# A mixture-of-experts kernel: each call's first block gets its second layer in the next call's code, and the next weights are fetched there

## Chip, cores, metric

One core of a Trainium2 chip. The metric is the device time in microseconds (us) from launch to the last output. The input is fixed, so the tokens of each expert are the same in every run.

## What is computed

Attention over q, k, v of 4 x 8 heads x 768 positions x 64, where each position sees its neighbours within 16 places and one summary (max of k, mean of v) of each block of 32. Its output, 3072 tokens of 512, goes through a mixture of 8 experts with one expert per token:

```python
logits = np.einsum('bsd,de->bse', x, w_gate)
local_gate = 1.0 / (1.0 + np.exp(-np.einsum('bsd,de->bse', x, w_local).squeeze(-1)))
...
            fresh_e = int(np.argmax(logits[b, s]))
            if s == 0 or local_gate[b, s] < 0.5:
                e = fresh_e
            else:
                e = prev_e if prev_e >= 0 else fresh_e
            prev_e = e
...
            h = np.maximum(x[b, s] @ w1[e], 0.0)
            out[b, s] = p[e] * (h @ w2[e])
```

w1[e] is 512 x 1024 and w2[e] 1024 x 512, so 4 MB of fp32 for one expert. The expert of a token can be that of the token before it, so the routing is known only on the chip.

## The kernel before, in words

Up to about 205 us the core does the attention, with the routing and the first expert blocks woven in by a hand-written planner (`flow`, `small`, `until`): small routing steps are generators that yield the name of the engine they use, and the constants C_T, C_LONG and the like say how much time a step takes up. After it, the work is a plain list.

Tokens are sorted by expert into blocks of 128. A *call* is one piece of code for 3 blocks (a 3-call), 2 blocks (a 2-call) or 1 block (`single`) of one expert. Which blocks are in use is known on the chip alone, so the calls stand in nests of branches: run's line 1525 for 3-calls 1 to 7, line 1533 for eight 2-calls, line 1539 for eight singles. When the count is reached, every engine jumps out of the nest, past the code of the calls that are not taken, and then catches up the semaphores that the skipped code would have counted. With this input the list is: early blocks of experts 2 and 3 within the attention; five 3-calls, three of expert 3 and two of expert 4; one 2-call of expert 2; one single of expert 6. Experts 0 and 6 also have a *few* part: up to 32 left-over tokens of an expert in a small block with its own weights (`few`, lines 1258 to 1295). The first few part stands behind 3-call 0, the second between the 3-calls and the 2-calls.

In a call (`blocks`), each fp32 product is three matmuls of split numbers, high times high, high times low and low times high. The first layer runs over 8 column groups f and 4 row groups c (lines 1187 to 1189, 96 matmuls), ACT applies the relu (line 1193) and DVE makes the low part (line 1195). The second layer runs block after block, 24 matmuls each (lines 1159 to 1161). After each block `store` scales by the gate (ACT line 1168 or DVE line 1171) and POOL writes the rows to their tokens by an indirect DMA (line 1172). Between the matmuls of the second layer stand the steps that get the next call ready: transposes of its tokens (`mid`, PE line 1138), and the *splits* of the next weights (`split`): ACT casts the high part (line 1113), DVE (line 1116) or POOL (line 1121) subtracts to get the low part. W1's four chunks are split in the first block's second layer, W2's in the last block's:

```python
SPLIT_BY = ("VGVV", "VGVG")
...
PW1, PW2 = (0, 2, 4, 6), (2, 4, 6, 7)
```

A split is under a branch on "the next call has new weights". Behind a matrix's last chunk SP fetches the weights after next into the staging tile `stg` (`refill`, `fetch` line 1109), two issues of 1 MB for each matrix. In all there are five such fetches; the last one names expert 0 by default and no call uses it.

The routing turns positions into gather lists: DVE writes the one-hot `bp` (lines 1042 to 1072) from `at`, a table of SLOTS block starts, and PE multiplies by it (line 1077).

Of the kernel before, what the change touches and what calls it, by code (L numbers as in the profile page):

```python
# [19 lines left out]
P = 128  # L20
# [15 lines left out]
N3, N2, N1, MORE = 8, 8, 8, 2  # L36
# [5 lines left out]
AT1 = AT2 + 2 * (N2 + MORE)  # L42
SLOTS = AT1 + N1 + MORE
# [29 lines left out]
C_LONG = {"LONG": 1.0, "LONGER": 1.8}  # L73
# [4 lines left out]
class Kernel:  # L78
# [755 lines left out]
    def finish(self):  # L834
# [146 lines left out]
        for i in range(2):  # L981
            yield "DVE"
            v.tensor_scalar(out=ends[:, i:i + 1], in0=pos[:, i, E:E + 1], scalar1=float(CALL), scalar2=None, op0=ALU.max)
# [5 lines left out]
        v.tensor_scalar(out=ends[:, 2:3], in0=pos[:, 2, E:E + 1], scalar1=float(CALL), scalar2=None, op0=ALU.max)  # L989
# [54 lines left out]
        yield "LONG"  # L1044
# [4 lines left out]
        for i in range(3):  # L1049
            yield "LONG"  # L1050
            v.tensor_tensor(out=bp[:, :, n * i:n * i + n], in0=eq, in1=self.p3[:, :, i, :].to_broadcast([P, NT, n]), op=ALU.mult)
# [56 lines left out]
    def fetch(self, dst, which, c0, c1, e):  # L1108
        self.nc.sync.dma_start(out=dst, in_=self.w[which][bass.ds(e, 1), :, c0:c1].rearrange("o p c -> (o p) c"))
# [14 lines left out]
    def gather(self, i):  # L1124
        t = self.xg[(i % 2, (i - EARLY) % CALL, (i - AT2) % 2, 0)[(i >= EARLY) + (i >= AT2) + (i >= AT1)]]
# [30 lines left out]
    def mm(self, ps, ah, al, w, first, last):  # L1156
        nc = self.nc
        wh, wl = w
        nc.tensor.matmul(out=ps, lhsT=ah, rhs=wh, start=first, stop=False)  # L1159
        nc.tensor.matmul(out=ps, lhsT=ah, rhs=wl, start=False, stop=False)  # L1160
        nc.tensor.matmul(out=ps, lhsT=al, rhs=wh, start=False, stop=last)  # L1161
# [13 lines left out]
    def blocks(self, i, k, mid, w1, w2, between=None):  # L1175
# [5 lines left out]
        for f in range(0, FT, per):  # L1181
            ps = self.bank("s")[:, 0:per * n].rearrange("p (f t) -> p f t", f=per)
            for j in range(per):
                for c in range(KT):
                    c0 = self.w1_at(f + j, c)
                    wh, wl = [w[0][:, c0:c0 + P] for w in (self.hi, self.lo)]
                    nc.tensor.matmul(out=ps[:, j], lhsT=wh, rhs=xh[c], start=(c == 0), stop=False)  # L1187
                    nc.tensor.matmul(out=ps[:, j], lhsT=wh, rhs=xl[c], start=False, stop=False)  # L1188
                    nc.tensor.matmul(out=ps[:, j], lhsT=wl, rhs=xh[c], start=False, stop=(c == KT - 1))  # L1189
# [6 lines left out]
        last = FT * (k - 1)  # L1196
        pm = PM if i else PM0
        for half in range(k):
            yp = self.bank("a")
            s = slice(P * half, P * half + P)  # L1200
            for f in range(FT):
                self.mm(yp, hT[:, f, 0, s], hT[:, f, 1, s], [x[1][:, f * DM:f * DM + DM] for x in (self.hi, self.lo)], f == 0, f == FT - 1)
                yield
                j = FT * half + f
# [4 lines left out]
                if between and j == FT * k - 4:  # L1209
                    between()  # L1210
                for at, w in (PW1, w1), ([last + x for x in PW2], w2):
                    if j in at:
                        w(*(q for q in range(4) if at[q] == j))
            self.store(yp, i + half, i < EARLY or half == k - 1)
        yield

    def single(self, i, mid, w1, w2):
# [16 lines left out]
        mm1(1, (2, 3))  # L1234
        w1(0, 1)
# [13 lines left out]
        self.store(yp, i)  # L1249
# [49 lines left out]
    def run(self):  # L1299
# [105 lines left out]
        def refill(w, nxt):  # L1405
            for h in range(2):
                self.fetch(st["stage"][w][:, 2048 * h:2048 * h + 2048], w, 2048 * h, 2048 * h + 2048, nxt)
# [6 lines left out]
        def calls(n, blocks, lane):  # L1414

            r = {}

            def start(s):
                while "words" not in st:
                    self.small(1, True)  # L1420
                if s not in r:
                    r[s] = reg(s, (ENG.SP, ENG.Activation, ENG.DVE, ENG.Pool), 1), reg(LANES + s, (ENG.SP,), E - 1)
                return r[s]

            def weights(w, chunks):
# [8 lines left out]
                new, nxt = start(lane)  # L1434
# [15 lines left out]
            return mid, lambda *chunks: weights(0, chunks), lambda *chunks: weights(1, chunks)  # L1450
# [9 lines left out]
        with ExitStack() as ctx:  # L1460
# [20 lines left out]
            def more_hT():  # L1481
# [3 lines left out]

            rest = chain(first, more_hT(), self.blocks(2, 2, *calls(4, 2, LANE1)), self.blocks(4, 2, *calls(EARLY, CALL, 0)),
                         self.blocks(EARLY, CALL, *calls(EARLY + CALL, CALL, 1), lambda: few_tx(0)))
# [24 lines left out]
            def few(j):  # L1512
                with tc.If(used[j] > 0):
# [8 lines left out]
            used = [few_reg(j, (ENG.PE, ENG.Activation, ENG.DVE, ENG.Pool)) for j in range(FEWS)]  # L1522
            few(0)
            n3, n2, n1 = [reg(2 * LANES + i, mybir.ALL_ENGINES, CALL * n) for i, n in enumerate((N3, N2, N1))]
            with ExitStack() as c:
                for n in range(1, N3):
                    c.enter_context(tc.If(n3 > CALL * n))
                    i = EARLY + CALL * n
                    for _ in self.blocks(i, CALL, *calls(i + CALL, CALL, n + 1)):
                        pass  # L1530
            few_tx(1)
            few(1)
            with ExitStack() as c:
                for n in range(N2):
                    c.enter_context(tc.If(n2 > CALL * n))
                    i = AT2 + 2 * n
                    for _ in self.blocks(i, 2, *calls(i + 2, 2, LANE2 + n + 1)):
                        pass
            with ExitStack() as c:
                for n in range(N1):  # L1540
                    c.enter_context(tc.If(n1 > CALL * n))
                    self.single(AT1 + n, *calls(AT1 + n + 1, 1, LANE3 + n + 1))

# [11 lines left out]
def consts():  # L1555
# [5 lines left out]
    at = [*range(EARLY, AT2), *(EARLY + CALL * n + h for n in range(N2 + MORE) for h in range(2)),  # L1561
          *(EARLY + CALL * n for n in range(N1 + MORE))]
# [71 lines left out]
```

## Time and profile before

| what | value |
|---|---|
| runs | 456.85, 456.86, 458.81 us; median 456.86 |
| profiled execution | 458.84 us, span first to last instruction 456.6 us |
| mean granted TensorE clock | 0.975 |
| busy share of the span | PE 92%, weight loads 80%, DVE 51%, ACT 42%, POOL 42% |
| weight fetches `stg` | 20 issues of 1 MB, median 7.1 us to landing |
| few-part weights `few_w` | 8 issues of 1 MB, median 8.5 us to landing |

The span is that of one profiled execution. Its time stands 1.98 us above the median of the runs. PE's busy share is the share of the span in which a matmul was in flight, so a PE at half clock counts as busy too. The granted clock is 1.00 at 2.4 GHz and 0.50 at 1.2 GHz. Rows with a q behind the engine's name (PEldq, DVEq) are the engine's sequencer: branches, semaphores, DMA issues.

### The profile page before, as it was taken

The page shows a single profiled execution, that of the slowest core. Times are in us where ns is not written, and L with a number is a line of the kernel's source. Part 1 is how long each engine was busy: PE and PEld are TensorE (multiplying, and loading weights), DVE is VectorE, ACT ScalarE, POOL GpSimd, SP SyncE. Part 2 cuts the span into 40 slices and gives each one's busy share as a digit, 9 for nine tenths or more (in the row PEclk, how much of TensorE's full clock was granted, in tenths as well). Part 3 has the DMA queues.
Part 4 walks back from the last instruction along what each step waited for, and adds up shares of the span by engine and source line. Part 5 has one row for each costly group of instructions (what it writes and reads, how often), then busy time and mean ns, then how long its engine had stood idle before and what let it go on. Part 6 is the DMA issues. An engine that isn't in the chain of part 4 may idle for free. (4 is left out here: it accounts for less than half of the span.)

```text
span 456.6 us, 11396 instructions
## 1 busy us (share of the span) xinstructions
PE 420.8 (92%) x4225; PEld 364.5 (80%) x4226; DVE 231.9 (51%) x581; ACT 190.3 (42%) x454; POOL 193.2 (42%) x287
## 2 busy tenths in 40 slices
PE   8799989899999999998999999999999999699084
PEld 4678868678897898988987988988988987597063
DVE  4766787998776789749331231244221244217001
ACT  4868787787752246221111221253320253127111
POOL 3687676688405209822033012034612024607601
PEclk9989999999999999999999999999999999899678
DMA  8999989997162900852484612006612006432901
GB/s 310 393 349 388 403 281 399 380 382 260 47 231 66 407 36 25 291 211 77 151 317 162 261 29 87 24 24 254 190 64 92 24 24 217 158 120 69 378 25 53
DMA packets 22855, 87.45 MB, mean 192 GB/s; under 512 B 2766, under 2 KB 3408, under 8 KB 19184
## 3 DMA queue, kind: packets, MB, share of 16 engines
q1 hardware_dynamic: 18176, 71.93, 42.3%
q0 software_dynamic: 4448, 14.29, 9.5%
q8 instruction: 39, 0.64, 0.6%
q14 instruction: 48, 0.39, 0.3%
q10 hardware_dynamic: 144, 0.20, 0.1%
HBM read 73.83 MB, written 12.71 MB: 190 GB/s over the span
## 5 line engine op out<-in xcount | busy, mean ns | idle before, releaser
L1187 PE MATMUL bs<-xT,h 128*128 128x384 f32 (+1 forms) x288 | 91.7, 319 | 0.8 <-issue 0.8
L1188 PE MATMUL bs<-xT,h 128*128 128x384 f32 (+1 forms) x288 | 89.9, 312 | 0.0
L1189 PE MATMUL bs<-xT,l 128*128 128x384 f32 (+1 forms) x288 | 89.8, 312 | 0.0
L1159 PE MATMUL ba<-h,hT 128*128 128x512 f32 x192 | 78.1, 407 | 0.0
L1127 POOL DMA_INDIRECT xg<-x_dram,gidx x30 | 30.5, 1018 | 106.3 <-PE bt L1138 55.7
L1161 PE MATMUL ba<-h,hT 128*128 128x512 f32 x192 | 75.4, 393 | 0.0
L1160 PE MATMUL ba<-l,hT 128*128 128x512 f32 x192 | 75.1, 391 | 0.0
L1195 DVE SCALAR_TENSOR_TENSOR hT<-bs,hT 128x384 fp32r<-128x384 f32 (+1 forms) x56 | 33.3, 594 | 82.1 <-ACT hT L1193 80.6
L1193 ACT ACTIVATE hT<-bs 128x384 fp32r<-128x384 f32 (+1 forms) x56 | 29.3, 523 | 100.9 <-PE bs L1189 99.0
L1187 PEld LDWEIGHTS bs<-xT,h 128*128 128x128 f32 x288 | 54.5, 189 | 2.1 <-issue 1.7
L1188 PEld LDWEIGHTS bs<-xT,h 128*128 128x128 f32 x288 | 54.6, 190 | 0.3
L1189 PEld LDWEIGHTS bs<-xT,l 128*128 128x128 f32 x288 | 54.5, 189 | 0.0
L1121 POOL TENSOR_TENSOR l<-stg,h 128x256 fp32r<-128x256 f32 x48 | 47.9, 1040 | 15.2 <-ACT h L1113 15.2
L317 ACT ACTIVATE pr<-bs,nm 128x120 f32<-128x120 f32 x192 | 50.9, 355 | 7.3 <-DVE nm L309 6.9
L1172 POOL DMA_INDIRECT out_dram<-yo,sidx x24 | 25.1, 1045 | 58.9 <-ACT yo L1168 12.3
L1161 PEld LDWEIGHTS ba<-h,hT 128*128 128x128 f32 x192 | 36.1, 188 | 7.9
L1160 PEld LDWEIGHTS ba<-l,hT 128*128 128x128 f32 x192 | 36.2, 189 | 6.3
L1159 PEld LDWEIGHTS ba<-h,hT 128*128 128x128 f32 x192 | 36.2, 188 | 6.3
L1113 ACT CAST h<-stg 128x1024 fp32r<-128x1024 f32 x32 | 33.2, 1050 | 17.7 <-PE ba L1161 16.6
L328 ACT COPY pt<-bt 124x384 f32<-124x384 f32 x64 | 27.8, 491 | 11.9 <-PE bt L327 11.8
L1116 DVE TENSOR_TENSOR l<-stg,h 128x1024 fp32r<-128x1024 f32 x20 | 26.1, 1303 | 13.2 <-ACT h L1113 13.1
L274 POOL COPY vw<-vs 24x384 f32<-24x384 f32 x64 | 30.3, 514 | 5.2 <-ACT vs L269 2.9
(264 smaller groups left out, 635.7 us busy)
## 6 DMA issues: line engine op xcount, KB each, us to landing
stg<-in_w SPq DMA_DIRECT2D x20, 1024.0 KB, 7.1
vw<-in_vW SPq DMA_DIRECT2D x16, 780.0 KB, 7.0
few_w<-in_w SPq DMA_DIRECT2D x8, 1024.0 KB, 8.5
kp<-in_kT SPq DMA_DIRECT2D x16, 384.0 KB, 6.2
q<-in_qT SPq DMA_DIRECT2D x16, 384.0 KB, 6.9
vt<-in_vT SPq DMA_DIRECT2D x16, 384.0 KB, 7.0
x_dram<-xs SPq DMA_DIRECT2D x8, 768.0 KB, 5.5
wst<-in_w SPq DMA_DIRECT2D x8, 512.0 KB, 7.0
```

The costliest lines, as they stand in the source:

```text
L274: nc.gpsimd.tensor_copy(out=vw[n % 3][WL:W, t:t + NW // 4, :, 0:D], in_=vs.to_broadcast([NB, NW // 4, 2, D]))
L317: nc.scalar.activation(out=pr[:, h, u, 0:W], in_=sp[:, h, u, :], func=AF.Exp, bias=nm[:, h, u:u + 1], scale=1.0)
L1113: self.nc.scalar.copy(out=hi, in_=src)
L1121: eng.tensor_tensor(out=lo[:, p], in0=src[:, p], in1=hi[:, p].bitcast(F32), op=ALU.subtract)
L1127: self.nc.gpsimd.indirect_dma_start(out=t, out_offset=None, in_=rows, in_offset=bass.IndirectOffsetOnAxis(ap=self.gidx[:, i:i + 1], axis=0))
L1159: nc.tensor.matmul(out=ps, lhsT=ah, rhs=wh, start=first, stop=False)
L1160: nc.tensor.matmul(out=ps, lhsT=ah, rhs=wl, start=False, stop=False)
L1161: nc.tensor.matmul(out=ps, lhsT=al, rhs=wh, start=False, stop=last)
L1187: nc.tensor.matmul(out=ps[:, j], lhsT=wh, rhs=xh[c], start=(c == 0), stop=False)
L1188: nc.tensor.matmul(out=ps[:, j], lhsT=wh, rhs=xl[c], start=False, stop=False)
L1189: nc.tensor.matmul(out=ps[:, j], lhsT=wl, rhs=xh[c], start=False, stop=(c == KT - 1))
L1195: nc.vector.scalar_tensor_tensor(out=l, in0=ps, scalar=0.0, in1=h.bitcast(F32), op0=ALU.max, op1=ALU.subtract)
```

## The change

The second layer of a call's first block leaves that call. It is now run by `left_over` as the first thing in the next call's code (in the code of the next 3-call, 2-call or single, whichever is taken), and W2's splits stand between its matmuls. A call's own second layer has the other blocks alone; W1's splits stand in the first of these. The next weights are fetched by `late`: SP issues all four pieces once the first group (f = 0) of the call's first layer is done on PE, by a dependency made by hand. `single` does this behind its first layer's last matmul. 3-calls 0 and 1 are always run (SURE = 2), and the second few part stands behind 3-call 1. ACT, in place of DVE, scales the left-over block and the single. The slot table grows by two (SLOTS 66 to 68): in front of the 2-calls and of the singles stands one more, the left-over block of the nest before. Two planner constants change and the one-hot steps are rated LONGER.

```diff
-N3, N2, N1, MORE = 8, 8, 8, 2
+N3, N2, N1, MORE, SURE = 8, 8, 8, 2, 2
...
-C_LONG = {"LONG": 1.0, "LONGER": 1.8}
+C_LONG = {"LONG": 0.9, "LONGER": 1.7}
...
-        yield "LONG"
+        yield "LONGER"
...
+    def left_over(self, i, w2=None):
+
+        def hook(f):
+            if w2 and f in PW2:
+                w2(PW2.index(f))
+
+        yield from self.second_layer(0, i, True, hook)
...
+            if refill and f == 0:
+                refill(ins)
+        halves = range(w2 is None, k)
+        pm, last = PM if i else PM0, FT * (len(halves) - 1)
+        for half in halves:
...
+            yield from self.second_layer(half, i + half, i < EARLY or half == k - 1, hook)
...
+        def late(lane):
+
+            def weights(after):
+                have_all()
+                new, nxt = reg(lane, (ENG.SP,), 1), reg(LANES + lane, (ENG.SP,), E - 1)
                 with tc.If(new > 0):
-                    split(w, chunks)
-                    if chunks[-1] == NCH - 1:
-                        refill(w, nxt)
+                    for w in range(2):
+                        refill(w, nxt, after)
...
+            def call3(n, between=None):
+                i = EARLY + CALL * n
+                if n:
+                    yield from self.left_over(i - CALL, splits(1, n))
+                yield from self.blocks(i, CALL, *calls(i + CALL, CALL, n + 1)[:2], None, between, late(n))
+
+            def call2(n):
+                i = AT2 + 1 + 2 * n
+                yield from self.left_over(i - (2 if n else 1), splits(1, LANE2 + n))
+                yield from self.blocks(i, 2, *calls(i + 2, 2, LANE2 + n + 1)[:2], None, None, late(LANE2 + n))
...
+            emit(call3(1, between1))
+            few(1)
...
+            def call1(n):
+                i = AT1 + 1 + n
+                self.single(i, *calls(i + 1, 1, LANE3 + n + 1), late(LANE3 + n))
+
+            with tc.If(n1 > 0) as some:
+                emit(self.left_over(AT1, splits(1, LANE3)))
+                call1(0)
...
+            with some.Else():
+                emit(self.left_over(AT1))
```

PE on leaving the 2-calls. `h_121` and `l_123` are the high and low parts of W2, `h_120` and `l_122` those of W1; L1533 and L1539 are the branches of the 2-calls and the singles. Before:

```order
L1159 MATMUL ba<-h_121,hT 128x512
L1160 MATMUL ba<-l_123,hT 128x512
L1161 MATMUL ba<-h_121,hT 128x512
L1435 UNCONDITIONAL_BRANCH
L1533 UNCONDITIONAL_BRANCH
L1533 UNCONDITIONAL_BRANCH [waits PE_49] x8
L1539 COMPARE_AND_BRANCH
L1159 MATMUL bs<-h_120,xT 128x512 [waits DVE_49,PE_49,Activation_49]
L1160 MATMUL bs<-l_122,xT 128x512 [waits DVE_49,Pool_49]
L1161 MATMUL bs<-h_120,xT 128x512 [waits DVE_49]
```

After (the branches are L1585 and, for the singles, L1594):

```order
L1454 UNCONDITIONAL_BRANCH
L1160 MATMUL ba<-l_123,hT 128x512 [waits Pool_49]
L1161 MATMUL ba<-h_121,hT 128x512
L1585 UNCONDITIONAL_BRANCH
L1585 UNCONDITIONAL_BRANCH [waits PE_49] x8
L1594 COMPARE_AND_BRANCH
L1159 MATMUL ba<-h_121,hT 128x512 [waits DVE_49,Activation_49]
L1160 MATMUL ba<-l_123,hT 128x512 [waits DVE_49]
L1161 MATMUL ba<-h_121,hT 128x512 [waits DVE_49]
L1159 MATMUL ba<-h_121,hT 128x512
L1160 MATMUL ba<-l_123,hT 128x512
```

What followed the jump before was the single's first layer, which needs the new W1 split by POOL; now it is 24 matmuls by the old W2, waiting for DVE and ACT only, with the splits of the new W2 among them.

SP around the first 2-call, its weight issues (`stg_3009` is W1's staging, `stg_3010` W2's). Before, behind the last chunk of each matrix in the 2-call's second layer:

```order
L1435 COMPARE_AND_BRANCH
L1109 ISA
L1109 DMA stg_3009<-in_w 128x2048 [waits DMAHW1_49,DVE_49,DMAHW5_49,Activation_49,Pool_49]
L1109 ISA
L1109 DMA stg_3009<-in_w 128x2048 [waits DMAHW6_49,DMAHW2_49,DVE_49]
L1435 UNCONDITIONAL_BRANCH
L1435 UNCONDITIONAL_BRANCH [waits DMAHW5_49,DMAHW6_49]
L1435 COMPARE_AND_BRANCH
...
L1435 COMPARE_AND_BRANCH
L1109 ISA
L1109 DMA stg_3010<-in_w 128x2048 [waits DMAHW3_49,DVE_49,DMAHW7_49,Activation_49,Pool_49]
L1109 ISA
L1109 DMA stg_3010<-in_w 128x2048 [waits DMAHW0_49,DVE_49,DMAHW4_49,Activation_49,Pool_49]
```

After, at the head of the same call, where `PE_49` among the waits is the first layer's first group:

```order
L1585 COMPARE_AND_BRANCH
L1422 TENSOR_LOAD words
...
L1454 UNCONDITIONAL_BRANCH x4
L1464 COMPARE_AND_BRANCH
L1109 ISA
L1109 DMA stg_3009<-in_w 128x2048 [waits DVE_49,DMAHW1_49,PE_49,DMAHW5_49,Activation_49,Pool_49]
L1109 ISA
L1109 DMA stg_3009<-in_w 128x2048 [waits DMAHW2_49,DMAHW6_49,DVE_49,Activation_49]
L1109 ISA
L1109 DMA stg_3010<-in_w 128x2048 [waits DMAHW3_49,DVE_49,DMAHW7_49,Activation_49,Pool_49]
L1109 ISA
L1109 DMA stg_3010<-in_w 128x2048 [waits DMAHW0_49,DVE_49,DMAHW4_49,Activation_49,Pool_49]
```

The four issues moved from two places in the second layer, each behind its own branch, to one place ahead of it, behind one branch and one wait for PE.

## Rows read from the trace of the kernel before

**Rows 1.** The page, span in 40 slices: granted TensorE clock in tenths.
```profile
PEclk9989999999999999999999999999999999899678
```

**Rows 2.** PE's waits: tile, line, releaser: us in total, times, longest.
```profile
PE bs L1159 <- DVEq L1533: 7.7, 1, 7.7
PE bs L1160 <- POOLq L1533: 4.8, 1, 4.8
PE bt L1265 <- DMA xg<-x_dram,gidx: 3.5, 1, 3.5
PE bt L1077 <- DVE bp L1072: 1.8, 1, 1.8
```

**Rows 3.** Timeline of PE, ACT, DVE: start us, length us, what [idle <-releaser].
```profile
387.49 0.39 PE L1161 MATMUL ba<-h,hT 128*128 128x512 f32 x1
...
398.44 0.39 PE L1187 MATMUL bs<-xT,h 128*128 128x256 f32 x1
...
410.06 0.40 PE L1159 MATMUL ba<-h,hT 128*128 128x512 f32 x1
...
421.70 0.39 PE L1161 MATMUL ba<-h,hT 128*128 128x512 f32 x1
...
435.31 0.80 PE L1160 MATMUL bs<-l,xT 128*128 128x512 f32 x1 [4.77 <-POOLq L1533]
...
449.54 0.39 PE L1161 MATMUL ba<-h,hT 128*128 128x512 f32 x1
...
390.70 0.69 ACT L1168 ACTIVATE yo<-ba,psort 128x512 f32<-128x512 f32 x1 [1.62 <-DMA out_dram<-yo,sidx]
...
421.89 1.23 DVE L1116 TENSOR_TENSOR l<-stg,h 128x1024 fp32r<-128x1024 f32 x1 [1.42 <-ACT h L1113]
```

**Rows 4.** Busy time by stretch; after POOL: granted clock, DMA share, GB/s.
```profile
241.80:249.80 8.00, 7.04 (x144) 5.56 (x144) 1.22 (x4) 1.24 (x3) 2.01 (x3) 1.00 0.39 129
249.80:284.30 34.50, 34.49 (x180) 31.44 (x181) 8.04 (x13) 5.70 (x11) 5.83 (x6) 1.00 0.36 141
392.30:395.70 3.40, 3.40 (x64) 3.19 (x63) 0.00 (x0) 0.28 (x1) 3.40 (x6) 0.51 0.21 77
422.10:435.30 13.20, 0.76 (x1) 0.29 (x1) 1.02 (x1) 1.63 (x2) 7.37 (x10) 0.67 0.92 349
436.00:440.00 4.00, 4.00 (x11) 3.14 (x10) 0.00 (x0) 0.00 (x0) 0.00 (x0) 0.50 0.01 4
440.00:450.00 10.00, 9.93 (x49) 7.83 (x48) 2.11 (x4) 2.96 (x5) 0.98 (x1) 0.99 0.06 17
```

**Rows 5.** PE's branches leaving 3-calls, 2-calls: ns min/median/max, first to last start.
```profile
L1525 PEldq COMPARE_BRANCH  x2: 184/3626/7068, 383.7 to 390.9; - x2
...
L1533 PEldq COMPARE_BRANCH  x2: 3586/4865/6144, 417.9 to 422.3; - x2
```

**Rows 6.** DMA issues (ns of the issue) and us to landing.
```profile
L1109 SPq DMA_DIRECT2D few_w<-in_w x4: 333/333/342, 246.4 to 249.2; - x4
...
DMA to landing us min/median/max: 5.0/8.5/10.9
...
L1172 POOL DMA_INDIRECT out_dram<-yo,sidx x1: 1026/1026/1026, 380.6 to 380.6; - x1
...
DMA to landing us min/median/max: 10.0/10.0/10.0
...
L1109 SPq DMA_DIRECT2D stg<-in_w x2: 343/439/535, 419.3 to 419.9; - x2
...
L1109 SPq DMA_DIRECT2D stg<-in_w x2: 332/332/332, 425.8 to 428.5; - x2
...
DMA to landing us min/median/max: 6.9/7.1/7.2
...
L1172 POOL DMA_INDIRECT out_dram<-yo,sidx x1: 1008/1008/1008, 451.0 to 451.0; - x1
...
DMA to landing us min/median/max: 3.2/3.2/3.2
```

More of the change, by code (lines that the diff above doesn't have):

```diff
@@ L1160, in mm @@
         nc.tensor.matmul(out=ps, lhsT=ah, rhs=wl, start=False, stop=False)
-        nc.tensor.matmul(out=ps, lhsT=al, rhs=wh, start=False, stop=last)
+        self.last_mm = nc.tensor.matmul(out=ps, lhsT=al, rhs=wh, start=False, stop=last).ins
     def store(self, yp, i, act=False):
@@ L1188, in blocks @@
                     nc.tensor.matmul(out=ps[:, j], lhsT=wh, rhs=xl[c], start=False, stop=False)
-                    nc.tensor.matmul(out=ps[:, j], lhsT=wl, rhs=xh[c], start=False, stop=(c == KT - 1))
+                    ins = nc.tensor.matmul(out=ps[:, j], lhsT=wl, rhs=xh[c], start=False, stop=(c == KT - 1)).ins
                     if k > 2 or c % 2:
@@ L1195, in blocks, with hook @@
             nc.vector.scalar_tensor_tensor(out=l, in0=ps, scalar=0.0, in1=h.bitcast(F32), op0=ALU.max, op1=ALU.subtract)
[L1196 to L1204, printed above, removed]
+            if refill and f == 0:
[3 more added lines that the diff above has]
+        for half in halves:
+            def hook(f):
+                j = FT * (half - halves[0]) + f
                 if i > EARLY and j == pm[0]:
@@ L1412, in split, with have_all, splits, weights @@
                 self.split(w, q * CH, q * CH + CH, st["stage"][w][:, q * CH:q * CH + CH], eng)
[L1414 to L1425, printed above, removed]
+        def have_all():
+            while "words" not in st:
+                self.small(1, True)
+        def splits(w, lane):
+            new = []
+            def weights(*chunks):
                 if lane is None:
@@ L1433, in weights, with calls @@
                     return
-                new, nxt = start(lane)
+                if not new:
+                    have_all()
+                    new.append(reg(lane, (ENG.Activation, ENG.DVE, ENG.Pool), 1))
+                with tc.If(new[0] > 0):
+                    split(w, chunks)
+            return weights
+        def late(lane):
+            def weights(after):
+                have_all()
+                new, nxt = reg(lane, (ENG.SP,), 1), reg(LANES + lane, (ENG.SP,), E - 1)
                 with tc.If(new > 0):
-                    split(w, chunks)
-                    if chunks[-1] == NCH - 1:
-                        refill(w, nxt)
+                    for w in range(2):
+                        refill(w, nxt, after)
+            return weights
+        def calls(n, blocks, lane):
             def mid(half):
@@ L1448, in mid @@
                         self.gather(n + half + blocks)
-            return mid, lambda *chunks: weights(0, chunks), lambda *chunks: weights(1, chunks)
+            return mid, splits(0, lane), splits(1, lane)
         def tick(G, point):
@@ L1535, in run @@
                     c.enter_context(tc.If(n2 > CALL * n))
[L1536 to L1542, printed above, removed]
+                    emit(call2(n))
+            def call1(n):
[4 more added lines that the diff above has]
+                call1(0)
+                with ExitStack() as c:
+                    for n in range(1, N1):
+                        c.enter_context(tc.If(n1 > CALL * n))
+                        call1(n)
+            with some.Else():
+                emit(self.left_over(AT1))
 def tile_kernel(tc, *args):
```

69 lines of the change are left out of this document (42 added, 27 removed).

## Prediction

> **What bounds the kernel now.** I read the page first. TensorE (PE) is busy for nearly the whole span, so only time in which PE stands still, or runs at its lower clock, can be won; the granted clock falls in the last slices alone [rows 1]. The list of PE's waits says where it stands still: behind DVE and then POOL as PE leaves the 2-calls, behind a gather at a few-token expert, and behind the routing's one-hot `bp` [rows 2]. PE's own rows around these waits give their limits [rows 3]. PE ends the last 3-call at 387.49 + 0.23 = 387.72 (0.23 is the distance between two 512-column matmuls) and begins the 2-call's first layer at 398.44: 10.72 us with one small expert in it. It ends the 2-call at 421.93 and begins the single block's second matmul at 435.31: 13.38 us for one matmul, so 13.15 lost. I then read the stretches [rows 4]: between 422.1 and 435.3 the DMA engines are busy for 0.92 of the time while PE has 0.76 us of work. Last come the branches of the skipped calls and the landings [rows 5, 6].
>
> A branch over skipped calls is cheap while little moves: PE's first one at 417.9 takes 3.59 us, ahead of its matmuls and so hidden. It is dear while a weight fetch runs: 7.07 us at 383.7, 6.14 at 422.3 [rows 5]. The stores say the same: 3.2 us to land with little else moving, 10.0 while the fetch of 379 runs [rows 6]. So the reading is that code and stores stand behind the weights. The Trainium skill ("Runtime: NRT & Kernel Launch", Instruction fetch mechanics) says that a taken branch to a page not yet held stalls until that page is fetched by DMA; the trace agrees as to the stall.
>
> **The change part by part**, against the profiled execution (458.84 us; its span is 456.6). The median of the three runs is 1.98 lower; I take that off at the end.
>
> *Routing one-hot.* `bp`'s matmuls stand behind nine more first-layer matmuls. A 3-call has 34.49/180 = 0.19 us per matmul [rows 4]: 1.7 us more cover for a wait of 1.8 [rows 2]. DVE's one-hots are some 3% longer and shift in DVE's order, so I leave 0.5: **-1.3** (bounds 0 and -1.8).
>
> *Leaving the 3-calls.* The split of the second layer's weights and the fetch no longer end the call; they are in the next call's code. What is late next is ACT's scaling of the last block (0.69 us, [rows 3]) and its hand-over, about 1.1 after PE's last matmul; PE's own branch runs ahead of its matmuls and is hidden if no weights move. They don't: the fetch starts in the call's first 3 us and needs 2.8 (246.4 to 249.2, the issues) + 10.9 = 13.7 us [rows 6] of a call of 34.5. Bounds 0.9 (hand-over alone) and the present 3.5 [rows 2]. The second small expert moves to behind the second 3-call. There it should cost what the first costs now: 241.8 to 249.8 less ten matmuls of the call before (2.25), 5.75 us [rows 4]; its weights are asked for a call earlier and hidden. New total 1.1 + 5.75 = 6.85 for 10.72: **-3.9**. This includes the clock, which stood at 0.51 for 3.4 us after the gather's wait [rows 4].
>
> *Leaving the 2-calls.* The last useful fetch starts after the first group of the 2-call's first layer: 24 of its 96 matmuls, 11.62/4 = 2.9 us in (398.44 to 410.06, [rows 3]). It is over at 2.9 + 13.7 = 16.6. The branch comes at 11.62 + half of 11.87 = 17.55, since one block instead of two is left [rows 3]. The margin is 0.9 us. PE's first hop is issued some 4 us ahead of its matmuls, still under weights; its second starts when the matmuls end (+0.35 now) and takes between 3.6 and 6.1 [rows 5]: PE is through after 4.0 to 6.5 us. DVE's last split there now ends 1.2 us after PE (421.89 + 1.23, [rows 3]); a split of the first layer's weights stands at the same place, and up to 1.1 later if ACT is behind; with a hop of 3.6 that is 3.6 (run ahead) to 5.9. I take **5.0** for 13.15: **-8.1**. Bounds 1.5 (all of it run ahead) and 7.7 (DVE as now [rows 2]). POOL isn't awaited there: the left-over block's first matmuls don't need it.
>
> *The single block's clock.* It now runs from 435.3 to 440.1 at half clock [rows 4], after 12.5 us with next to no work: 4.8 us of time for 2.4 of work, **-2.4**. But a stop of 3.5 us was enough for a fall before [rows 2, 4], and 5.0 is longer; it is paid once in the left-over block, 3.4 us at half clock: **+1.7** (bounds 0 and 2.4).
>
> *Block 0's second layer.* Its matmuls only change place: 0. They are the cover for the splits, which now sit inside them, with 21 or more us of first layer before their results are read.
>
> *The late fetch.* SP's branch and four issues lie beside PE; the first half lands within 7 us and the second layer begins 16.7 us later in a 3-call, 11.6 in a 2-call. 0 in the middle. At the end it isn't: the last fetch serves no call, and now ends at 435.7 (419.3 and on), ahead of the last block's matmuls. It will start half way through the single block and end 13.8 us later, some 8 us after PE's last matmul. The last store stands behind it. Today 6.4 us follow PE's end, 3.2 of them this landing [rows 6]. A landing of 10.0 instead would give +6.8, the fetch's own end plus what now follows the landing (456.5 - 454.2 = 2.3) gives 8.1 + 2.3 = 10.4, +4.0. With one more branch level (0.3) and the exit's code behind weights I take **+5.0** (bounds +1 and +9).
>
> Sum: -1.3 - 3.9 - 8.1 - 2.4 + 1.7 + 5.0 = -9.0. 458.84 - 9.0 = 449.84, less 1.98: **447.9 us**. Its own range, with each jump and the tail 1.5 us off, is 444 to 451.
>
> **The rivals.**
> *A, better.* The hops run ahead and the 2-calls are left after 2.5 us, the clock does not fall, and the tail costs 3: -2.5 - 1.7 - 2.0 more, 441.7. For it: the idle of 1.8 us before `bp`'s matmuls left the clock at full [rows 1, 2]. Against: DVE's split.
>
> *B, the hops stay dear.* If a code load takes 6 to 7 us whatever else moves, the exits stay at 3.5 and 7.7 us: +2.4 + 2.7, **453.0**. For it: the dear hops are also those whose engine had other work queued. Against: the first hop at 417.9 and the store's 3.2. The Trainium skill ("DMA: Bandwidth & Descriptors", Queues, rings and completion order) has each DMA engine take its queues in turn, a packet at a time; by that, code on its own queue would not stand behind megabytes of weights, moving the fetch would not shorten a hop, and this rival would be the case. The rows of 7.07 against 3.59 speak against it.
>
> *C, slower.* The fetch begun late is still in flight at the jump out of the 2-calls: every engine's hop then loads behind it, the stop stays at 13.15 with its clock, and the useless fetch lengthens the tail by the full 9: 458.84 - 1.3 - 3.9 + 9 - 1.98 = **460.7**. It decides at the 0.9 us margin above: a fetch that ends over 2 to 3 us later than 16.6 brings it. For it: the fetch of 419 needed 16.4 in all, because its second half waited for splits (425.8, 428.5 [rows 6]). Against: in the new place no issue waits for a split.
>
> *D, the change doesn't do what it says* for the small expert: at its new place its tokens or weights are late, and the stop of 3.5 us [rows 2] and the half clock's 1.7 stay: +5.2, **453.1**. Against: the first small expert shows no such wait in its stretch [rows 4], and 34.5 us of call lie before the second.
>
> **How the numbers follow.** Forecast 0.55, A 0.14, B 0.20, C 0.06, D 0.05. The range 441 to 454.5 leaves out the lower part of A, the upper of B and all of C, some 0.16. A measurement of this kernel can tell 0.5% (2.3 us) from no change. Faster by more needs under 454.6: forecast, A, most of B and D, 0.88. Within 2.3 us: the dear ends of B and the mild ones of C, 0.06. Slower: the rest of C and a tail past its bound, 0.06.
>
> **What would show it.** In the new profile: PE's wait for `bp` under 1 us; the small expert behind the second 3-call in about 5.8 us at full clock; PE's wait on leaving the 3-calls near 1, on leaving the 2-calls near 5, with the weights' landings before that branch; stores landing in about 3 us at both exits; the last `stg` issues half way through the single block, and the last store landing 7 to 10 us after its issue. The prediction is wrong if the hops take 6 us with no weights in flight (B), if the weights land after the branch out of the 2-calls (C), or if the tail after PE's last matmul stays near 6.4 us, in which case the time is nearer A's.

## The result and the profile after

The changed kernel takes 450.65 us (median of four runs, 450.15 to 451.44), the kernel before 457.81 beside it: a ratio of 0.9845, interval 0.9812 to 0.9878. In a second comparison, with six runs, it was 0.9873, 0.9817 to 0.9928. So the change makes the kernel some 1.4% faster. A run over 1.5% above the fastest of its kernel is left out of the ratios; there is one, of 457.94 us, in the eighth experiment. The profiled execution took 451.44 us, its span went from 456.6 to 449.7. Three words are used below: the *exit* of a nest is the place where the engines leave it; a *hop* is the time from an engine's branch out of a nest to its first instruction behind it; the *tail* is the time from PE's last matmul to the end of the span.

The page of the changed kernel, the granted clock in 40 slices; it answers to [rows 1]:

```profile
PEclk9989999999999999999999999999999999899795
```

PE's waits in the changed kernel (tile, line, releaser: total us, times, longest), for [rows 2]. The waits for `bp`, for the gather, and of 7.7 and 4.8 us are gone; at the exits of the two nests two of 3 us, both for ACT's sequencer, and one of 0.5 are left:

```profile
PE ba L1159 <- ACTq L1585: 3.0, 1, 3.0
PE ba L1159 <- ACTq L1581: 2.9, 1, 2.9
...
PE ba L1160 <- DVEq L1585: 0.5, 1, 0.5
```

PE's timeline (start us, length us, what), for [rows 3]. PE ends the last 3-call at 383.80 + 0.23 = 384.03 and starts the left-over block 3.05 us later; it ends the 2-call at 412.22, and starts 3.17 us later with a second short stop behind the first matmul. Its last matmul ends at 436.85:

```profile
383.80 0.39 PE L1161 MATMUL ba<-h,hT 128*128 128x512 f32 x1
387.08 0.50 PE L1159 MATMUL ba<-h,hT 128*128 128x512 f32 x1 [2.90 <-ACTq L1581]
...
394.28 0.28 PE L1205 MATMUL bs<-xT,h 128*128 128x256 f32 x1
...
411.99 0.40 PE L1161 MATMUL ba<-h,hT 128*128 128x512 f32 x1
415.39 0.79 PE L1159 MATMUL ba<-h,hT 128*128 128x512 f32 x1 [3.01 <-ACTq L1585]
416.64 0.79 PE L1160 MATMUL ba<-l,hT 128*128 128x512 f32 x1 [0.45 <-DVEq L1585]
...
436.46 0.39 PE L1161 MATMUL ba<-h,hT 128*128 128x512 f32 x1
```

Busy time by stretch of the changed kernel (us, then busy us and instructions of PE, PEld, DVE, ACT, POOL, then granted clock, DMA share, GB/s), for [rows 4]. Behind the first exit the clock is at half for about 3.4 of 7.2 us, behind the second for the whole of 6.3 us; the single, which ran its first 4.8 us at half clock before, now has 0.99; and behind PE's last matmul lie 12.8 us:

```profile
387.00:394.20 7.20, 7.12 (x24) 5.71 (x25) 1.23 (x1) 3.14 (x3) 2.23 (x3) 0.76 0.12 45
...
415.40:421.70 6.30, 5.85 (x13) 4.28 (x14) 1.23 (x1) 1.04 (x1) 1.74 (x2) 0.50 0.27 90
421.70:428.40 6.70, 6.70 (x30) 5.53 (x30) 1.23 (x1) 4.33 (x5) 5.40 (x7) 0.99 0.00 1
...
436.90:449.70 12.80, 0.00 (x0) 0.00 (x0) 0.00 (x0) 0.69 (x1) 1.01 (x1) 0.58 0.64 235
```

What moved at the two exits and at the end, for [rows 5, 6]: ACT's last scaling before the first exit and its first semaphores behind it, then the issues with their us to landing, and PE's branch. The last useful fetch begins 3.6 us into the 2-call's first layer and has landed after 14.4 us (397.9 to 399.9 + 12.4), at 412.3: with PE's last matmul of the 2-call, no earlier. The last fetch (431 to 447) lies over the tail, PE's branch out of the singles' nest takes 6.1 and 6.2 us, and the last store 9.1 us to land:

```profile
384.27 0.69 ACT L1168 ACTIVATE yo<-ba,psort 128x512 f32<-128x512 f32 x1 [4.20 <-PEq L1581]
...
L1581 ACTq EVENT_SEMAPHORE  x2: 17/17/17, 387.0 to 387.1; - x2
...
L1109 SPq DMA_DIRECT2D stg<-in_w x4: 333/335/383, 397.9 to 399.9; - x4
...
DMA to landing us min/median/max: 5.1/9.7/12.4
...
L1109 SPq DMA_DIRECT2D stg<-in_w x4: 333/333/343, 430.7 to 432.7; - x4
...
DMA to landing us min/median/max: 5.1/10.0/14.2
...
L1597 PEldq COMPARE_BRANCH  x2: 6119/6182/6246, 433.7 to 440.2; - x2
...
L1172 POOL DMA_INDIRECT out_dram<-yo,sidx x1: 1009/1009/1009, 437.9 to 437.9; - x1
...
DMA to landing us min/median/max: 9.1/9.1/9.1
```

### The profile page after: what moved, and what is told of

It reads as the page before. It is cut to its first block, busy times and chain, and to the rows that moved or that the text cites. A ratio compares the mean times of both kernels' runs of the same rounds, so it can differ in the third digit from the quotient of the medians.

```text
span 449.7 us, 11359 instructions
## 1 busy us (share of the span) xinstructions
PE 420.9 (94%) x4225; PEld 363.9 (81%) x4226; DVE 227.6 (51%) x574; ACT 195.2 (43%) x461; POOL 194.4 (43%) x287
## 5 line engine op out<-in xcount | busy, mean ns | idle before, releaser
L1159 PE MATMUL ba<-h,hT 128*128 128x512 f32 x192 | 80.5, 419 | 5.9 <-ACTq L1585 3.0
L1160 PE MATMUL ba<-l,hT 128*128 128x512 f32 x192 | 76.7, 399 | 0.5 <-DVEq L1585 0.5
L1161 PE MATMUL ba<-h,hT 128*128 128x512 f32 x192 | 76.9, 401 | 0.0
L1121 POOL TENSOR_TENSOR l<-stg,h 128x256 fp32r<-128x256 f32 x48 | 49.2, 1054 | 24.6 <-ACT h L1113 24.6
L1159 PEld LDWEIGHTS ba<-h,hT 128*128 128x128 f32 x192 | 37.2, 194 | 13.8 <-ACTq L1585 3.5
L1161 PEld LDWEIGHTS ba<-h,hT 128*128 128x128 f32 x192 | 36.9, 192 | 8.4
L1160 PEld LDWEIGHTS ba<-l,hT 128*128 128x128 f32 x192 | 37.3, 194 | 7.5 <-DVEq L1585 1.0
L1113 ACT CAST h<-stg 128x1024 fp32r<-128x1024 f32 x32 | 33.2, 1049 | 19.6 <-PE ba L1161 18.6
L1168 ACT ACTIVATE yo<-ba,psort 128x512 f32<-128x512 f32 x19 | 13.0, 687 | 54.3 <-PE ba L1161 50.1
```

Source lines behind the costliest of these rows:

```text
L1113: self.nc.scalar.copy(out=hi, in_=src)
L1121: eng.tensor_tensor(out=lo[:, p], in0=src[:, p], in1=hi[:, p].bitcast(F32), op=ALU.subtract)
L1161: self.last_mm = nc.tensor.matmul(out=ps, lhsT=al, rhs=wh, start=False, stop=last).ins
```

## The experiments

They ran in three sets, each beside its own runs of the kernel before, and each ratio is to these: the first four experiments (median of before 459.19 us), the next four (457.00), the last three (459.45).

### No useless fetch

```diff
                 new, nxt = reg(lane, (ENG.SP,), 1), reg(LANES + lane, (ENG.SP,), E - 1)
-                with tc.If(new > 0):
+                with ExitStack() as c:
+                    if more is not None:
+                        c.enter_context(tc.If(more))
+                    c.enter_context(tc.If(new > 0))
                     for w in range(2):
...
-                self.single(i, *calls(i + 1, 1, LANE3 + n + 1), late(LANE3 + n))
+                self.single(i, *calls(i + 1, 1, LANE3 + n + 1), late(LANE3 + n, n1 > CALL * (n + 1)) if n < N1 - 1 else lambda after: None)
```

> The change with one edit: a single block fetches weights only if a further single follows, so the last 4 MB, which no call uses, are not moved. Theory: the tail behind PE's last matmul grew from 6.7 to 12.9 us because the last store and the engines' exit code stand behind that fetch; without it the tail is 6.2 to 7.5 us, PE's last branch takes about 3.6 us in place of 6.1, the last store lands in about 3 us, and the time is 444 to 445. Rival: the longer tail is the deeper nest of branches of the changed kernel; then it stays above 11 us and the time above 449. Everything ahead of the single block is as in the changed kernel.

Measured: ratio 0.9733 (0.9678 to 0.9788), span 443.9; the median is 446.61 us, 1.6 over the forecast, beside runs of before that stand 1.4 higher than those of the first comparison. PE's branch out of the nest of singles (ns min/median/max, first and last start), and PE's last matmul:

```profile
L1600 PEldq COMPARE_BRANCH  x2: 3139/3232/3326, 433.6 to 437.2; - x2
...
436.37 0.39 PE L1161 MATMUL ba<-h,hT 128*128 128x512 f32 x1
```

The tail is 443.9 - 436.76 = 7.1 us in place of 12.85, and the branch takes 3.1 and 3.3 us in place of 6.1 and 6.2. The jump out of the same nest takes half the time once the weights are gone. That is what the Trainium skill ("DMA: Bandwidth & Descriptors", Queues, rings and completion order) would not lead one to expect, since it lets each DMA engine serve its queues in turn; here the jump beside weights takes twice as long, by whatever way. The Trainium skill ("Runtime: NRT & Kernel Launch", Instruction fetch mechanics) says that a taken branch to a page not yet held stalls until that page is fetched; the trace agrees as to a stall, 3.1 and 3.3 us with no weights in flight. The landing of the last store isn't in this trace, so how the tail's gain divides between jump and store is not shown.

### Matmuls of no use behind the nests

```diff
-        for n, k, side in ("a2", 1, "left"), ("s0", 1, "left"), ("s1", 2, "right"):
+        for n, k, side in ("a2", 1, "left"), ("s0", 1, "left"), ("s1", 1, "right"), ("fill", 1, "right"):
...
+    def fill(self, n):
...
+        for _ in range(n):
+            self.nc.tensor.matmul(out=self.fill_bank, lhsT=self.ones, rhs=self.A[:, 0:4, :].rearrange("p a b -> p (a b)"), start=True, stop=True)
...
+                if not n:
+                    self.fill(12)
                 yield from self.left_over(i - (2 if n else 1), splits(1, LANE2 + n))
...
             with tc.If(n1 > 0) as some:
+                self.fill(12)
                 emit(self.left_over(AT1, splits(1, LANE3)))
```

> The change with one edit: PE gets twelve 512-column bf16 matmuls of no use (some 2.6 us, into a PSUM bank that nobody reads) behind each of the two nests of branches, ahead of the left-over block; the first layer gives up one of its three PSUM banks for that. Theory: the granted clock falls at both exits because PE stands still for 3 us, and costs 1.7 us in the first left-over block and 3.3 in the second. With the fill the clock stays at 1.00 through both, the 24 matmuls behind the 3-calls take 5.5 us in place of 7.2, and the time falls by 3.5 to 5 us, to 445.7 to 447. Rival 1: the fall has another cause (what the other engines or the DMA do); then 0.50 shows again at both places and the time stays within 1 us. Rival 2: two banks are too few for the first layer; then its 96 matmuls take longer than 16.7 us in each 3-call.

Measured: ratio 0.9812 (0.9776 to 0.9847), span 447.1. Stretches, columns as above: the left-over block behind the 3-calls, then the one behind the 2-calls with the single's first matmuls:

```profile
388.20:393.80 5.60, 5.60 (x26) 4.65 (x25) 1.23 (x1) 3.13 (x3) 1.77 (x3) 1.00 0.15 56
...
415.30:425.50 10.20, 9.98 (x44) 7.94 (x43) 2.45 (x2) 5.38 (x6) 4.38 (x7) 1.00 0.18 56
```

The clock stays at 1.00 in both, and the 24 matmuls behind the 3-calls take 5.65 us (388.23 to 393.88). From the matmul behind the last call's last transposes to the first layer of the 2-call, the first exit takes 1.5 us less than in the change (13.65 against 15.12); from the same place in the 2-call to the single's first transposes, the second takes 2.5 us less (15.23 against 17.74). The sum, 4.0, is in the range expected, but the span shows 2.6, and the runs do not show it clear of noise: their median is 449.88 us where 445.7 to 447 was expected, and the interval of the ratio overlaps that of the change. The other rival, two banks being too few, is out: a 3-call's first layer takes 16.67 us as before.

### The fetch back in its old place

```diff
                 with tc.If(new[0] > 0):
                     split(w, chunks)
+                    if chunks[-1] == NCH - 1:
+                        refill(w, new[1])
...
-                with tc.If(new > 0):
-                    for w in range(2):
-                        refill(w, nxt, after)
+                pass
```

> The change with one edit undone: the next weights are fetched behind each matrix's last split (W1 in the second layer, W2 in the left-over block) as before, and not behind the first group of the first layer. Theory: 2 MB of weights are then in flight at both exits, hops of 2.7 to 3.5 us become 5 to 7, PE stands still for 5 to 8 us at each exit in place of 2.9 and 3.5; the useless last fetch ends earlier and the tail falls back to 7 to 9 us. Sum about +5 to +8 at the exits and -4 to -6 in the tail: 449 to 455. Rival (code has a queue of its own and takes its turn): the stops stay at 3 us at both exits, and the time falls by the tail alone to about 445.

Measured: ratio 0.9981 (0.9957 to 1.0005), about 458 us: nearly all of the gain is gone, more than expected, though the tail fell to 7.0 us as expected. PE's waits at the exit of the 3-calls (branch L1582), in the single and at the exit of the 2-calls (branch L1586), POOL's stores at the first exit, ACT's wait at the second, SP's catch-up there (ns min/median/max, first and last start), and ACT's hop at the first:

```profile
PE ba L1160 <- POOLq L1582: 6.1, 1, 6.1
PE bt L1138 <- ACT hs L1247: 4.0, 1, 4.0
PE ba L1159 <- ACTq L1586: 3.1, 1, 3.1
...
386.95 1.02 POOL L1172 DMA_INDIRECT out_dram<-yo,sidx  x1 [0.30 <-issue]
...
397.33 1.02 POOL L1172 DMA_INDIRECT out_dram<-yo,sidx  x1 [8.08 <-DMA out_dram<-yo,sidx]
...
ACT h L1113 <- SPq L1586: 13.1, 1, 13.1
...
L1586 SPq EVENT_SEMAPHORE  x9: 17/17/17, 430.7 to 435.1; - x9
...
L1582 ACTq COMPARE_BRANCH  x2: 38/44/50, 388.9 to 389.7; - x2
...
L1582 ACTq EVENT_SEMAPHORE  x2: 17/17/17, 389.6 to 389.7; - x2
```

The place of the fetch decides, but not by the step that was expected. At the first exit PE, ACT and DVE jump as the weights begin to flow, in 3.6 us or less, ACT in 0.7. By the waits, what is dear is to catch up: POOL and SP pass only when their own transfers have landed. At the first exit POOL's store waits 8.1 us for the landing of the one before it, which was issued at 386.95, behind the weights of 385.5; POOL's catch-up stands behind that store, and PE's eighth matmul of the left-over block needs it: a stop of 6.1 us. At the second exit PE stops for ACT as in the change (3.1 us). SP catches up from 430.7 to 435.1, behind the weights issued at 423.9, with the DMA engines busy to about 433; the splits in the left-over block wait 13.1 us for SP, and PE then 4.0 for the ACT that they made late. So at these exits it was landings that others had to wait for, and not a jump, that the weights made dear. This is read from one trace; no experiment takes the catch-up away by itself.

### Without the last block's scaling

```diff
-        self.store(yp, i, act)
+        if keep:
+            self.store(yp, i, act)
...
-            yield from self.second_layer(half, i + half, i < EARLY or half == k - 1, hook)
+            yield from self.second_layer(half, i + half, i < EARLY or half == k - 1, hook, not (i > EARLY and half == k - 1))
```

> The change, leaving out the gate scaling and the store of the last block of each 3-call and 2-call (those rows of the output stay unwritten). Theory: PE's stop behind the 3-calls is ACT's own hop of 2.7 us, which ACT can issue only when the scaling of the last block, its last work, has begun. Without that work ACT's branch is done before PE's last matmul, the stop falls from 2.9 us to under 1 us, and the clock stays at 1.00 there. Behind the 2-calls DVE still has a split to end and its own hop, so PE's stop there stays at 3 to 4.5 us, named DVE, and the clock falls. Time about 447. Rival (PE's own hop or POOL's catch-up sets the stop): 2.9 us and the half clock remain behind the 3-calls.

One run, 446.39 us. PE's waits in this kernel:

```profile
PE ba L1159 <- DVE l L1116: 1.8, 1, 1.8
...
PE ba L1160 <- DVEq L1586: 1.3, 1, 1.3
...
L1586 ACTq EVENT_SEMAPHORE  x2: 17/17/17, 411.7 to 411.8; - x2
```

At the exit of the 3-calls 0.7 us of idle is left, named for nobody but PE: the stop of 2.9 us in the change was ACT's hop behind its last scaling. (The edit takes POOL's store away too, but the stop was named for ACT, not for POOL.) Behind the 2-calls there are 1.8 us named DVE, at whose end (411.78) ACT's catch-up falls too, its hop having begun at 409.1 behind its last cast, and then 1.3 us for DVE's hop. Together 3.1, as the theory said. The clock, against expectation, stays at 1.00 there too: these two stops of under 2 us, a matmul between them, did not bring a fall.

### Both edits together

The edits of the first two experiments, unchanged.

> The change with the edits of the first two experiments together: no fetch in a single block that no further single follows, and twelve matmuls of no use behind each nest of branches. In the profiled executions the one took the span from 449.7 to 443.9 us, the other to 447.1. Theory: they act in different places (tail; clock behind the exits) and add up: span 440 to 442, time some 8 us under the change's, clock 1.00 up to PE's last matmul. Rival: what PE gains at the exits is given back, since the tail's length is set by something else that ends at a fixed time; then it is no faster than without the fill.

Measured: ratio 0.9665 (0.9628 to 0.9702), span 442.5 in the slowest of its five runs, median 441.47. Within the intervals they add up; the profiled execution, the slowest, is 0.5 us over the span expected.

### The late fetch alone

```diff
+            if refill and f == 0:
+                refill(ins)
         last = FT * (k - 1)
...
                 with tc.If(new > 0):
                     split(w, chunks)
-                    if chunks[-1] == NCH - 1:
-                        refill(w, nxt)
...
-                    for _ in self.blocks(i, 2, *calls(i + 2, 2, LANE2 + n + 1)):
+                    for _ in self.blocks(i, 2, *calls(i + 2, 2, LANE2 + n + 1), None, late(LANE2 + n)):
```

> The kernel before with one part of the change alone: the weights are fetched behind the first group of a call's first layer. The left-over block and the new place of the small expert are not in it, so W2's splits stay at the end of a call. Theory: the late fetch needs the left-over block to pay: at the exit of the 2-calls POOL has W2's splits until some 6.5 us behind PE's last matmul and then its own hop, and the next first layer needs POOL, so PE stands still for 8 to 11 us there (13.2 before, about 4 in the change); the stop behind the 3-calls stays at about 3 us; and the tail pays the useless fetch, +6. Sum +0 to +4 against before. Rival: the late fetch is the whole gain (without it the change is as slow as before); then PE's stop behind the 2-calls is under 5 us and the time within 3 us of the change's.

Measured: ratio 0.9937 (0.9903 to 0.997), a small gain where a loss of up to 4 us was expected. PE's waits behind its 2-calls (branch L1548):

```profile
PE bs L1159 <- ACTq L1548: 4.1, 1, 4.1
...
PE bs L1160 <- POOLq L1548: 2.8, 1, 2.8
```

6.9 us of stop behind the 2-calls in place of 12.5, under the 8 to 11 expected, as POOL no longer waits beside weights. But it is nearly twice the stop of the change, and the tail pays the useless fetch: 13.1 us in place of 6.7. By its time the rival is not far off: 453.66 us is 2.5 to 3.8 us above the change, reckoned by the change's two ratios; by its other sign, a stop under 5 us, it is out. Together with the third experiment this says that in whole time neither half of the change does much alone: the late fetch 0.6%, all the rest without it 0.2% (an interval that takes in no gain at all), both 1.3 to 1.6%. But the tail hides what the late fetch does. In the profiled executions, one of each kernel, PE's last matmul ends at 449.9 us before, at 442.2 with the late fetch alone, at 451.1 with the rest alone and at 436.9 with both: up to there the late fetch is worth most of the gain, and the rest needs it.

### The small expert back in its old place

```diff
-                few_tx(1)
+                pass
...
             emit(call3(1, between1))
-            few(1)
...
                     emit(call3(n))
+            few_tx(1)
+            few(1)
             with ExitStack() as c:
```

> The change with the second small expert back in its old place, behind the 3-calls' nest. Theory: the place is worth little, because the stop there is ACT's hop behind its last scaling, which comes all the same, and the half clock behind it then falls on the small expert's matmuls in place of the left-over block's: within 1.5 us of the change. Rival (the prediction's step): the place saves the stop and the half clock of the small expert, 2 us or more.

Measured: ratio 0.9769 (0.973 to 0.9809), 446.6 us: faster than the change by more than either theory had. PE's timeline across the exit of the 3-calls, and ACT's:

```profile
379.78 0.39 PE L1161 MATMUL ba<-h,hT 128*128 128x512 f32 x1
380.71 0.40 PE L1284 MATMUL bt<-ident,few_x 32*128 32x32 f32 x4 [0.54 <-PEq L1580]
381.49 1.95 PE L1299 MATMUL bs<-few_w,few_xT 128*32 128x128 f32 x64 [0.38 <-DVE few_xT L1285]
383.61 0.57 PE L1303 MATMUL bt<-ident,few_h 128*128 128x128 f32 x2 [0.16 <-ACT few_h L1300]
384.32 1.96 PE L1310 MATMUL ba<-few_w,few_hT 128*32 128x128 f32 x64
386.20 0.50 PE L1159 MATMUL ba<-h,hT 128*128 128x512 f32 x1
...
380.25 0.69 ACT L1168 ACTIVATE yo<-ba,psort 128x512 f32<-128x512 f32 x1 [4.21 <-PEq L1580]
383.27 0.52 ACT L1300 ACTIVATE few_h<-bs 128x128 f32<-128x128 f32 x2 [2.33 <-ACTq L1580]
```

The stop is 0.54 us. The small expert's transposes need PE's own catch-up and DVE's, not ACT's; ACT's hop (380.3 to 382.9) is over just as the first half of the matmuls is there for its relu. The small expert is 5.5 us of work for PE that needs ACT late, at the one place where ACT is late, and the clock stays up. From the end of the last 3-call to the first layer of the 2-call this kernel takes 391.79 - 380.01 = 11.78 us with the small expert, the change 394.28 - 384.03 = 10.25 without it, and 5.1 for it elsewhere. The change's 10.25 holds 1.7 for the half clock; in the repeated run of the change below, where the clock stayed up, the same stretch takes 8.7. So the cover is worth 3.5 us where the clock falls behind the stop, 2.0 where it doesn't.

### The planner's constants

```diff
-C_LONG = {"LONG": 0.9, "LONGER": 1.7}
+C_LONG = {"LONG": 1.0, "LONGER": 1.8}
...
-        yield "LONGER"
+        yield "LONG"
```

> The change with the planner's constants and the one-hot steps' rating as before. Theory: these set how many first-layer matmuls stand ahead of the routing's one-hot matmuls (66 in the change, 57 or 58 before); with them undone PE's wait of about 1.8 us for `bp` is back, and the time is 1 to 2.5 us over the change's. Rival: the wait went with something else (fewer early steps on DVE); then PE's list of waits shows no `bp` and the time is the change's.

Measured: ratio 0.9886 (0.9822 to 0.995), three runs from 449.97 to 454.36. PE's wait is back:

```profile
PE bt L1077 <- DVE bp L1072: 1.9, 1, 1.9
```

The wait is shown, and in this execution the stretch from the first layer's start to the second layer takes 21.6 us, against 19.6 in the change and 21.4 before. In the time of the runs this price is inside the spread: the ratio's interval overlaps both of the change's.

### The change again, and two kernels that beat it

The kernel of the change unchanged; the edits of the first and the seventh experiment together; and these with the `fill(12)` of the second ahead of the single's left-over block only.

> The change itself once more, on one chip with the two kernels below, since the time of the kernel before and of its variants has differed by one or two per mille between chips and the last comparisons are of kernels from different sets of runs. Expected: the ratio of the first comparison, 0.981 to 0.988 of before. Were it near 0.977, the small expert's old place would be worth nothing.

> The change with the small expert back behind the 3-calls' nest and without the last, useless fetch. Theory: at its old place the small expert's matmuls wait for nothing of ACT's but its own relu, so they cover ACT's hop: 4 us under the change; without the last fetch the tail is some 6 us shorter. Together 8 to 10 us under the change, ratio to before 0.962 to 0.967, with no twelve matmuls of no use. Rival: the small expert's gain was a difference between chips; then it stays at some 6 us under the change, as the first experiment.

> The kernel of the line above with twelve matmuls of no use ahead of the left-over block of the single alone, where no small expert covers the exit. Theory: the stop of 3 us there no longer lets the clock fall to half (which costs 1.5 to 3.3 us in the traces so far): 2 to 3 us under the kernel above, ratio to before 0.956 to 0.962, clock 1.00 up to PE's last matmul. Rival: the fall of the clock shifts from there to a later stretch; then both kernels have the same time.

Measured: the change 0.9873 (0.9817 to 0.9928), 453.24 us; the second kernel 0.9663 (0.9619 to 0.9707), 444.40; the third 0.963 (0.9583 to 0.9677), 442.62. The small expert's place and the useless fetch are worth 8.8 us beside the change, as expected. The matmuls of no use are worth another 1.8 us of median, a little under the 2 to 3 expected, and the intervals overlap; but at their place the traces differ as much: from the matmul behind the 2-call's last transposes to the single's first, 409.00 to 425.94 without, 409.33 to 424.50 with. The third kernel's clock, the stretch behind the 2-calls of the second and of the third kernel, and the stretch behind the 3-calls of the repeated change:

```profile
PEclk9989999999999999999999999999999999999997
...
414.00:425.90 11.90, 11.02 (x41) 8.90 (x42) 2.47 (x2) 5.38 (x6) 6.76 (x9) 0.86 0.15 48
...
414.40:424.50 10.10, 9.98 (x44) 7.90 (x43) 2.95 (x2) 5.38 (x6) 5.54 (x7) 1.00 0.19 58
```

```profile
388.00:393.50 5.50, 5.50 (x24) 4.56 (x25) 1.23 (x1) 3.14 (x3) 1.74 (x3) 1.00 0.15 55
```

In this execution of the change the stop behind the 3-calls was 2.92 us, as in the first (2.90), and the clock stayed at 1.00 for the whole left-over block; in the first it fell. So a stop of this length does not always bring a fall. With six runs each, the two kernels with a covered exit vary less from run to run: 443.96 to 444.60 and 441.59 to 444.74 against 450.29 to 456.95.

## Why the prediction was right, and where not

The time fell by 7.2 us beside its own runs of before, where 9.0 was forecast, and 450.65 lies in the range of 441 to 454.5 and in the forecast's own of 444 to 451. The direction and the places held. The sum came this near in part by luck: errors of 3.0, 1.5 and 1.2 us to the bad stand against 1.4 and 0.5 to the good and a gain of 1.9 that was not foreseen. By terms, in the two profiled executions:

| term | forecast | measured |
|---|---|---|
| routing one-hot | -1.3 | -1.8 |
| leaving the 3-calls, with the small expert | -3.9 | -0.9 |
| leaving the 2-calls | -8.1 | -9.5 |
| the single's half clock | -2.4 | -2.4 |
| the clock behind the 2-calls | +1.7 | +3.2 |
| tail | +5.0 | +6.2 |
| first small expert, attention part | 0 | -1.9 |

The one-hot term is the time from 204.51 to 225.94 before, 203.51 to 223.13 now. The 3-calls' exit was 10.72 with the small expert, and is 10.25 less some 5.5 for the left-over's 24 matmuls at full clock plus 5.07 for the small expert (5.75 was forecast), 9.8. The tail went from 6.67 (449.93 to 456.6) to 12.85.

**Leaving the 3-calls** is the step that failed: "PE's own branch runs ahead of its matmuls and is hidden", with ACT's hand-over of 1.1 us last. PE's branch was hidden, but ACT has one of its own, it can issue that only when its last scaling has begun, and 2.7 us later it goes on (384.3 to 387.0, in the fence on the exits above): the experiment without the scaling shows it. I had read [rows 5] for PE alone. Yet ACT's rows of the kernel before would not have given 2.7 us either: there the hop took 0.7.

```profile
L1525 ACTq COMPARE_BRANCH  x2: 38/44/50, 390.7 to 391.6; - x2
L1525 ACTq EVENT_SEMAPHORE  x2: 17/17/17, 391.4 to 391.5; - x2
```

It took 0.7 us in the third experiment too, beside weights, and 1.3 with the late fetch alone. So at this exit the change made ACT's hop some 2 us longer; by what, no run shows. The clock fell behind the stop, which cost 1.7 us in this execution. Worse, the price set on moving the small expert had the wrong sign: it was counted as part of a gain, and the seventh experiment shows that its old place was the cover for ACT's hop, worth 3.5 us there (10.25 + 5.07 - 11.78), or 2.0 where the clock holds.

**Leaving the 2-calls** was mis-sized, to the good: 3.2 + 0.5 us in place of 5.0, since ACT's hop (412.5 to 415.3) was last and DVE's came only just behind. PE's second branch, priced at 3.6 to 6.1 us, took 0.2, and its first, 4.5 beside the end of the fetch, was over at 413.1:

```profile
L1585 PEldq COMPARE_BRANCH  x3: 85/186/4500, 384.6 to 413.3; - x3
```

The fetch landed at 412.3, not 0.9 us ahead of the jump but with PE's last matmul, so rival C was near. Its mechanism, hops that load behind the weights, is not what the third experiment shows: with weights in flight at the first exit the hops there stayed short, and landings were what PE waited for.

**The clock behind the 2-calls** was mis-sized: half clock for 6.7 us (415.0 to 421.7), twice the row of 3.4 that it was taken from.

**The tail** was right in cause, shown by the first experiment, and 1.2 us short: the store landed in 9.1 us, and 2.7 more followed.

**Rival B** fell: PE's hops out of the fetch's way took no more than 4.1 us in any of these traces, and those out of the last nest went from 6.1 and 6.2 to 3.1 and 3.3 with the fetch alone taken away. Rival D fell too: the small expert has no wait and full clock at its new place. That was never what it cost.

Two parts of the change were not tried alone: ACT in DVE's place for scaling the left-over block and the single, and the second 3-call taken out of the branches. The terms add up to -7.1 of the span's -6.9. The two gains of 1.9 at the end were not foreseen. 0.9 is a wait of PE's behind the first small expert that is gone with the code that followed; that cause was not tried. The rest is not shown to be the change's: up to the end of the attention the traces of these kernels differ by up to 3.8 us (the same first layer begins at 203.2 to 207.0, before at 204.5, in two executions of the change at 203.5 and 203.2).

## What to carry to other kernels

Where engines jump over code, list each engine's last instruction before its jump, and what the first instruction behind the jump needs of whom: the engine with the latest last instruction sets the stop, and work that doesn't need that engine belongs there. Keep large transfers out of the few microseconds around a jump and around the end, where stores have to land before anyone goes on; a prefetch that nobody uses is not free when it stands ahead of the last store. Before moving a piece of work out of a gap because it waits there, ask what it covers.

## What was not expected of the hardware

Over all these traces PE's jump over code cost 3.1 to 4.1 us with no fetch beside it or only the start of one, 4.2 to 4.8 beside the end of a weight fetch, and 5.7 to 7.1 beside a whole one. ACT's hop at the exit of the 3-calls took 2.7 us in the change and 0.7 in the kernel before and in the third experiment, there beside weights; why is open. A store of 256 KB landed in 2.8, 3.2 and 3.6 us with little in flight, in 9.1 and 10.0 beside weights. A stop of PE of 2.9 us brought half clock in one execution of the same kernel and none in another; eleven or twelve cheap matmuls in the stop kept it at 1.00 each time it was tried.
